# Weights converted at the start of an attention, MLP and expert kernel: exponents rebased by ScalarE, a normalisation's factor kept in a PSUM bank, and sixteen of the lower parts made by TensorE with identities

## The chip, the core and the metric

One core of one Trainium2 chip. The metric is the device time of one execution in microseconds (us). TensorE multiplies matrices into PSUM (eight banks, of which this kernel shares some), VectorE and ScalarE work element by element from SBUF and PSUM, GpSimd does so from SBUF alone, and SyncE starts transfers. In the profile's rows the engines are called PE, PEld (the load of TensorE's weights), DVE (VectorE), ACT (ScalarE), POOL (GpSimd) and SP (SyncE).

## The reference

Eight batches of 576 positions. First an attention without scores between positions, in eight heads of 64; its result, seen as 576 x 512, goes through a layer normalisation and an MLP of 512 to 2048 to 512 with a residual; then two of four small causal attentions are chosen for each position and mixed.

```python
q_s = softmax(q, axis=-1);  k_s = softmax(k, axis=seq)
kv = np.einsum('bhsd,bhse->bhde', k_s, v)
x = np.einsum('bhsd,bhde->bhse', q_s, kv)          # to (8, 576, 512)
xn = (x - mu) / np.sqrt(var + 1e-06) * g_ln
x = x + np.maximum(xn @ w_ch1, 0.0) @ w_ch2        # 512 -> 2048 -> 512
...                                                # top 2 of 4 experts of causal attention
```

## The kernel before

A batch is worked on in two halves of 288 columns. A unit is a pair of heads, four to a batch: its `k` and `q` are loaded, the exponentials taken, `q` is turned by products with an identity (`pq`), the product `pkv` is made and scaled into `kvw`, and a product of each half (`po`, plain fp32 while the unit is one of the first eight) is copied into `xT` by ScalarE. Norm is the layer normalisation of a half: GpSimd adds up the four parts of `xT` (`x_sum`), ScalarE and VectorE split the sum in two (`lnsum`), TensorE takes the mean of it (`pmu`), VectorE subtracts it (`xc`), ScalarE squares (`sq`), the same again gives the variance (`pvar`), three operations on ScalarE and two on VectorE (`refine`) give the factor, `scale` multiplies with it and with the gain, and ScalarE and VectorE split the outcome into a high and a lower part (`xhl`).

The MLP's matrices come in blocks of 128 rows by 512 as 64-bit floats. Each block is turned by `Wide.pieces` into a float32 that is split into a high part (f32r, the form that TensorE takes in one pass) and a lower part; three products (high with high, high with low, low with high) make one exact enough product. Block 2f is the part of the first matrix for step f (`w1_f`), block 2f+1 that of the second (`w2_f`). A step of the MLP is twelve products into `psh`, ReLU and split into `hh` by ScalarE and VectorE, and twelve products into four accumulators `acc0` to `acc3`.

The function `start` lays out batch 0's units, its norms and its first pass through steps 0 to 11 (in two chunks, 0 to 6 and 7 to 11, each for both halves), the conversion of blocks 0 to 23, and batch 1's units and norms. It names every operation with its engine, an assumed cost and what it depends on; rings say how many tiles or banks of a kind there are and who has to be done before the next one is handed out (`y`: two PSUM banks; `t`: four tiles of 128x512, in which blocks are converted and `x_sum` is kept; `raw`: four raw blocks). A greedy planner makes one order of it for each engine, and `in_order` holds every engine to that order. Later batches follow a fixed pattern; the last eight blocks are converted in the last pass by `Wide.step`. `CDVE` names the blocks whose lower part VectorE makes; GpSimd makes the others.

The pieces of a block, in the kernel's own words (the raw block's `low` and `high` are the two words of each number):

```python
nc.scalar.activation(t.bitcast(F32), high.bitcast(F32), AF.Abs)                                  # size
nc.vector.tensor_scalar(t, t, TINY, None, op0=ALU.max)                                           # least
nc.vector.tensor_scalar(t, t, 3, 0x3FFFFFF8, op0=ALU.logical_shift_left, op1=ALU.bitwise_and)    # shift
nc.scalar.activation(low, low.bitcast(U32), AF.Copy, scale=2.0 ** -29)                           # rest
nc.vector.scalar_tensor_tensor(box[0], high, -0x40000000, box[0], ...)                           # sign
nc.gpsimd.tensor_tensor(box[0], box[0], low, op=ALU.add)                                         # whole
nc.scalar.activation(h, box[0].bitcast(F32), AF.Copy)                                            # big
eng.tensor_tensor(lo, box[0].bitcast(F32), raw(h), op=ALU.subtract)                              # small
```

Of the kernel before, what the change touches and what calls it, by code (L numbers as in the profile page):

```python
# [7 lines left out]
F32 = mybir.dt.float32  # L8
# [18 lines left out]

WHOLE, KPOOL, QACT = 8, (0, 1, 5, 6, 7), (0, 1, 6, 7)

CDVE = (1, 4, 7, 8, 9, 14, 16, 17, 18, 20, 21)  # L30

DIRECT = ((0, 0),)

# [9 lines left out]
UNIT_AT, UNIT_GAP = (0, 1, 2, 4, 5, 7), 4  # L43
NORM_AT, NORM_GAP = (0, 2, 4, 6, 8, 10), 8

TINY = 2.0 ** -15 * 1.125


def weave(main, side):
# [80 lines left out]
def tile_kernel(ctx: ExitStack, tc: tile.TileContext, q, k, v, g_ln, w1, w2, w_gate, wq, wk, wv, wo, out):  # L130
# [25 lines left out]
    def raw(ap):  # L156
        return ap.bitcast(F32)
# [15 lines left out]
    def mm(o, lhsT, rhs, start, stop):  # L173
        nc.tensor.matmul(o, lhsT, rhs, start=start, stop=stop)  # L174
# [22 lines left out]
    mean_r = const.tile([P, P], F32R, name="mean_r")  # L197
    nc.vector.memset(raw(mean_r), 1.0 / DM)
    mean_mat = raw(mean_r)
    eps6 = const.tile([P, 1], F32, name="eps6")  # L200
    nc.vector.memset(eps6, 1e-6)
    g_sb = const.tile([P, NDC], F32, name="g_sb")
# [11 lines left out]
    class Wide:  # L214
# [18 lines left out]
        def pieces(self):  # L233


            r, h, lo = self.now()
            n = self.at
            self.at += 1
            low, high = r[:, :, 0], r[:, :, 1]
            box = []  # L240

            def size():
                t = self.pool_t.tile([P, DM], I32, tag="t", name="w_t", bufs=TB)
                box.append(t)
                nc.scalar.activation(t.bitcast(F32), high.bitcast(F32), AF.Abs)

            def least():
                t = box[0].bitcast(F32)
                nc.vector.tensor_scalar(t, t, TINY, None, op0=ALU.max)

            def shift():
                t = box[0]
                nc.vector.tensor_scalar(t, t, 3, 0x3FFFFFF8, op0=ALU.logical_shift_left, op1=ALU.bitwise_and)

            def rest():
                nc.scalar.activation(low, low.bitcast(U32), AF.Copy, scale=2.0 ** -29)

            def sign():
                nc.vector.scalar_tensor_tensor(box[0], high, -0x40000000, box[0], op0=ALU.bitwise_and,  # L259
                                               op1=ALU.bitwise_or)  # L260

            def whole():
                nc.gpsimd.tensor_tensor(box[0], box[0], low, op=ALU.add)  # L263

            def big():
                nc.scalar.activation(h, box[0].bitcast(F32), AF.Copy)

            def small():
                eng = nc.vector if n in CDVE else nc.gpsimd
                eng.tensor_tensor(lo, box[0].bitcast(F32), raw(h), op=ALU.subtract)  # L270
                while len(self.tiles) < min(n + 1 + self.ahead, len(self.blocks)):
                    self.load()

            return size, least, shift, rest, sign, whole, big, small

        def now(self):
            while len(self.tiles) <= self.at:
# [2 lines left out]

        def step(self):
            if self.at < len(self.blocks):
                for piece in self.pieces():
                    piece()

    def fc_blocks(f, w1t, w2t):
# [305 lines left out]
    class Norm:  # L592
# [37 lines left out]
        def less(self, c, n):  # L630
            if c == 0:
                self.xc = lp.tile([P, NDC, T], F32, tag="xc", name="xc")
            nc.vector.tensor_tensor(self.xc[:, c:c + n], self.xs[:, c:c + n],
                                    self.pmu[:, None].to_broadcast([P, n, T]), op=ALU.subtract)
# [12 lines left out]
        def refine(self):  # L647

            r0, t = (self.sq[:, i] for i in (1, 2))
            nc.vector.scalar_tensor_tensor(t, self.pvar, 1e-6, t, op0=ALU.add, op1=ALU.mult)  # L650
            nc.vector.scalar_tensor_tensor(t, t, 3.0, r0, op0=ALU.subtract, op1=ALU.mult)

        def scale(self, c):
            xc = self.xc[:, c]
            nc.vector.scalar_tensor_tensor(xc, xc, g_sb[:, c:c + 1], self.sq[:, 2], op0=ALU.mult, op1=ALU.mult)

        def high(self, c, n):
            if c == 0:
# [167 lines left out]
    def start():  # L826
# [117 lines left out]
        def norm(b, h):  # L944
# [7 lines left out]
            def mean(nm, x, done, add_, buf):  # L952
                if direct:
                    ps = op = None
                    for c in range(NDC):
                        op = A((nm, c), PE_, 490, lambda c=c: u.mean_direct(nm, x, c), [done[c], op])
                        ps = ps or op
                    return ps, op
                op = None
                for c in range(1, NDC):  # L960
                    op = A((nm, "add", c), POOL, 750, lambda c=c: add_(c), [op, done[0], done[c]])
                    if c == 1 and buf:
                        op0 = op
                hi = A((nm, "high"), ACT, 330, u.sum_high, [op])
                lo = A((nm, "low"), DVE, 370, u.sum_low, [hi])
                if buf:
                    op0.take(buf, lo)
                ps = A((nm, "mean"), PE_, 240, lambda: u.mean(nm), [lo])
                hi.take("lnsum", ps)
                return ps, ps  # L970

            first, last = mean("pmu", lambda: u.xs, kp, u.add_x, "t")
            less, sq = [], []
            for c in range(0, NDC, n):
                less += [A(("less", c), DVE, 370 if direct else 670, lambda c=c: u.less(c, n), [last, less[-1] if less else None])] * n
# [2 lines left out]
            first, last = mean("pvar", lambda: u.sq, sq, u.add_sq, None)  # L978
            root = A("root", ACT, 1000, u.root, [last])
            fine = A("fine", DVE, 800, u.refine, [root, at["g2"]])  # L980
            first.take("m" if direct else "y", fine)
            sc, lo = [], None
            his = []
            for c in range(NDC):
                sc.append(A(("sc", c), DVE, 430, lambda c=c: u.scale(c), [fine]))
                if (c + 1) % n == 0:
                    hi = A(("hi", c), ACT, 330 if direct else 570, lambda c=c: u.high(c + 1 - n, n), sc[c + 1 - n:] + his[-1:])
                    his.append(hi)
                    lo = A(("lo", c), DVE, 370 if direct else 670, lambda c=c: u.low(c + 1 - n, n), [hi, lo])
            less[0].take("xc", lo)  # L990
            sq[0].take("sq", sc[-1])
            at["hl", b, h] = lo

            his[0].take("xhl", *([at["lastf", h]] if b == 0 else ()))
# [3 lines left out]
        for k in range(nblocks):  # L998
            box = []
            live.append(box)  # L1000
            A = lambda nm, eng, cost, fn, deps: add(("w", k, nm), eng, cost, fn, deps)

            def one(i, box=box):
                if not box:
                    box.extend(wide.pieces())
                box[i]()

            g = lambda i, one=one: (lambda: one(i))
            ld = add(("w", k, "ld"), SP, 1450, wide.load, [at.get(("w", k - 1, "ld"))], lat=1100)
            c0 = A(0, ACT, 520, g(0), [at.get(("w", k - 1, 0)), ld])  # L1010
            c1 = A(10, DVE, 340, g(1), [c0])
            c1 = A(1, DVE, 340, g(2), [c1])
            c2 = A(2, ACT, 520, g(3), [c0])
            c3 = A(3, DVE, 600, g(4), [c1])
            c5 = c4 = A(4, POOL, 1220, g(5), [c2, c3])
            c6 = A(6, ACT, 520, g(6), [c4])
            c7 = A(7, *((DVE, 600) if k in CDVE else (POOL, 1220)), g(7), [c6, at.get(("w", k - 1, 7))])
            c0.take("t", c7)
            ld.take("raw", c5)

# [595 lines left out]
```

## Time and profile before

| | |
|---|---|
| median of 3 runs | 1355.34 us (1354.69 to 1357.6) |
| the profiled execution | 1356.32 us, its span 1354.6 us |
| mean granted clock of TensorE | 0.992 |
| TensorE busy | 1297.1 us (96%) |
| VectorE busy | 889.6 us (66%) |
| ScalarE busy | 687.5 us (51%) |
| GpSimd busy | 342.4 us (25%) |
| TensorE in 40 slices of the span, tenths | 5678 and then 35 times 9, at the end 7 |

The shares are means over the whole execution. A slice is 34 us long. Only the first four slices and the last show TensorE with room, so what happens there is read from windows and timelines of the first 164 us and not from the shares. The first `psh` of the MLP begins at 46.73 us; the stages below are cut there and at later groups of products. A row of a timeline is a run of equal instructions on one engine; behind it stands in brackets how long the engine was idle before it and which operation ended that. Matmuls are pipelined, so a row's length includes the drain of its last one; the distance between starts tells what a group takes.

### The profile page before, as it was taken

Reading aid. Unit: us, or ns where it says so; the run is one execution under the profiler, and the core shown is the slowest. Engines: PE = TensorE matmul, PEld = TensorE weight load, DVE = VectorE, ACT = ScalarE, POOL = GpSimd, SP = SyncE. Lnnn points to the kernel's source line nnn. Section 1 sums busy time; section 2 is a strip of 40 time slices with the busy share of each in tenths; the row PEclk is TensorE's granted clock in tenths of the full one; section 3 lists DMA queues with packets and bytes.
Section 4 is the critical chain, followed back from the end, with each engine's and each line's share of the span. In section 5 each row is a group of like instructions: output and inputs, shape, how many; then the busy total and the mean of one; then the engine's idle time right before and its main releaser. Section 6 shows DMA issues by size and latency. Waiting matters only on the chain.

```text
span 1354.6 us, 26863 instructions
## 1 busy us (share of the span) xinstructions
PE 1297.1 (96%) x9932; PEld 1255.8 (93%) x9932; DVE 889.6 (66%) x2602; ACT 687.5 (51%) x1802; POOL 342.4 (25%) x445
## 2 busy tenths in 40 slices
PE   5678999999999999999999999999999999999997
PEld 3578999999999999999999999999999999999995
DVE  7999564654645656456472238777768677776785
ACT  7667443434343434344442135656556656565666
POOL 5756413122131221212240002111211111121211
PEclk9898999999999999999999999999999999999999
DMA  8655232331322324215112023323232332423021
GB/s 228 200 174 150 80 96 72 112 93 50 110 75 94 85 72 114 75 53 156 64 34 47 1 83 121 107 83 106 85 94 90 90 98 62 118 84 86 23 67 56
DMA packets 136772, 124.84 MB, mean 92 GB/s; under 512 B 84160, under 2 KB 124096, under 8 KB 133056
## 3 DMA queue, kind: packets, MB, share of 16 engines
q1 hardware_dynamic: 126176, 97.16, 25.6%
q10 hardware_dynamic: 10464, 25.95, 5.3%
q8 instruction: 79, 1.29, 0.4%
q14 instruction: 53, 0.43, 0.1%
HBM read 74.07 MB, written 35.39 MB: 81 GB/s over the span
## 4 chain that ended last, share of the span: by engine, by line
PE 70%; DVE 4%; DMA 2%; ACT 1%; issue 1%; SPq 0%; POOL 0%; ACTq 0%; DVEq 0%
PE psh L174 21%; PE acc L174 14%; PE psqk L174 7%; PE psc L174 7%; PE pssc L174 4%; PE py L174 4%; PE psv L174 4%; PE pso L174 3%; PE pst L1401 2%; PE po L174 1%; DMA q<-in_q_dram 1%; PE pkv L174 1%; PE pst L1450 1%; DMA k<-in_k_dram 0%; PE pq L510 0%
## 5 line engine op out<-in xcount | busy, mean ns | idle before, releaser
L174 PE MATMUL psh<-xhl,w 128*128 128x288 f32 x3072 | 470.4, 299 | 5.2 <-DVE w L270 2.2
L174 PEld LDWEIGHTS psh<-xhl,w 128*128 128x128 f32 x3072 | 429.7, 190 | 8.6 <-DVE w L270 2.5
L174 PE MATMUL acc<-hh,w 128*128 128x288 f32 x2400 | 371.4, 299 | 10.0 <-DVE hh L714 8.9
L174 PEld LDWEIGHTS acc<-hh,w 128*128 128x128 f32 x2400 | 335.6, 189 | 14.4 <-DVE hh L714 10.9
L714 DVE SCALAR_TENSOR_TENSOR hh<-psh,hh 128x288 fp32r<-128x288 f32 x200 | 90.5, 453 | 159.5 <-ACT hh L711 158.2
L711 ACT ACTIVATE hh<-psh 128x288 fp32r<-128x288 f32 x200 | 81.6, 408 | 170.0 <-PE psh L174 165.2
L1389 POOL TENSOR_SCALAR sm<-sm,st,lg 128x128 f32<-128x128 f32 (+3 forms) x128 | 80.3, 637 | 273.6 <-DVE st L1386 99.1
L174 PE MATMUL psqk<-x,wqk 128*128 128x288 f32 x768 | 112.6, 298 | 0.5 <-DVE lg L1289 0.3
L174 PEld LDWEIGHTS psqk<-x,wqk 128*128 128x128 f32 x768 | 104.7, 188 | 1.8 <-PE pst L1401 0.8
L174 PE MATMUL psc<-hb,w 128*128 128x288 f32 x672 | 100.5, 299 | 0.0
L1377 ACT ACTIVATE sm<-sm,st 128x128 f32<-128x128 f32 (+2 forms) x144 | 83.7, 583 | 17.9 <-DVE st L1369 16.7
L174 PEld LDWEIGHTS psc<-hb,w 128*128 128x128 f32 x672 | 92.4, 189 | 0.3
L1420 ACT ACTIVATE aTh<-pst 128x128 fp32r<-128x128 f32 (+5 forms) x254 | 79.2, 334 | 24.7 <-PE pst L1401 12.2
L1369 DVE CUSTOM_DVE_ANT_0 sm<-pssc,mask 128x128 f32<-128x128 f32 (+2 forms) x144 | 67.7, 482 | 32.2 <-PE pst L1401 19.9
L1421 DVE TENSOR_TENSOR aTl<-pst,aTh 128x384 fp32r<-128x384 f32 (+4 forms) x222 | 82.0, 382 | 9.8 <-ACT aTh L1420 7.1
L476 POOL TENSOR_TENSOR qe<-q,sm 128x320 f32<-128x320 f32 x64 | 47.5, 763 | 87.5 <-PE pkv L515 78.2
L611 POOL TENSOR_TENSOR sq<-sq 128x288 f32<-128x288 f32 x45 | 37.3, 828 | 109.4 <-ACT sq L639 107.4
L174 PE MATMUL py<-aTh,vv 128*128 128x320 f32 (+4 forms) x228 | 58.4, 275 | 1.6 <-DVE yf L1473 0.9
L425 POOL TENSOR_TENSOR q<-q,sm 128x640 f32<-128x640 f32 x28 | 35.9, 1283 | 91.2 <-DVE sm L422 86.2
L174 PE MATMUL pssc<-k,q 128*128 128x128 f32 (+3 forms) x256 | 58.0, 326 | 0.5 <-DVE st L1369 0.5
L263 POOL TENSOR_TENSOR w_t<-w_t,wraw 128x512 int32<-128x512 int32 x32 | 45.2, 1414 | 51.6 <-DVE w_t L259 13.3
L174 PE MATMUL psv<-wvg,x 128*128 128x260 f32 (+1 forms) x384 | 54.3, 285 | 0.0
(174 smaller groups left out, 2115.8 us busy)
## 6 DMA issues: line engine op xcount, KB each, us to landing
wraw<-in_moe_w_ch_dram SPq DMA_DIRECT2D x32, 512.0 KB, 3.9
xn_d<-xhl ACTq DMA_DIRECT2D x14, 1152.0 KB, 5.0
xhl<-xn_d SPq DMA_DIRECT2D x14, 1152.0 KB, 5.1
xp_d<-xT ACTq DMA_DIRECT2D x16, 576.0 KB, 3.6
k<-k SPq DMA_DIRECT2D x32, 288.0 KB, 3.5
k<-in_k_dram SPq DMA_DIRECT2D x32, 256.0 KB, 2.9
q<-in_q_dram SPq DMA_DIRECT2D x32, 256.0 KB, 3.6
out_dram<-ot SPq DMA_DIRECT2D x32, 256.0 KB, 2.0
```

The lines of the kernel that those rows point to most:

```text
L174: nc.tensor.matmul(o, lhsT, rhs, start=start, stop=stop)
L263: nc.gpsimd.tensor_tensor(box[0], box[0], low, op=ALU.add)
L425: nc.gpsimd.tensor_tensor(self.q3, self.q3, self.sm[:, 0, :, None].to_broadcast([P, 2 * NCH, D]), op=ALU.subtract)
L476: nc.gpsimd.tensor_tensor(self.qe[:, :, j, :], self.qt[:, j], self.sm[:, 2, j * NCH:(j + 1) * NCH, None].to_broadcast([P, NCH, D]), op=ALU ...
L611: nc.gpsimd.tensor_tensor(self.t, self.t, self.sq[:, c], op=ALU.add)
L711: nc.scalar.activation(self.hh[:, 0], self.ps, AF.Relu)
L714: nc.vector.scalar_tensor_tensor(self.hh[:, 1], self.ps, 0.0, raw(self.hh[:, 0]), op0=ALU.max, op1=ALU.subtract)
L1369: nc.vector.tensor_tensor_reduce(out=sm[:m, c0:c1], in0=o_, in1=msk, scale=1.0, scalar=3e38 if n == 0 else st[:m, j, 0:1], op0=ALU.add, op ...
L1377: nc.scalar.activation(sm[:m, :w], sm[:m, :w], AF.Exp, bias=st[:m, j, last:last + 1], scale=-1.0, accum_out=st[:m, j, 2:3])
L1389: nc.gpsimd.tensor_scalar(sm[:m, :w], sm[:m, :w], st[:m, j, 3:4], self.gate()[:, j:j + 1], op0=ALU.mult, op1=ALU.mult)
L1420: nc.scalar.activation(oh, from_, AF.Copy)
L1421: nc.vector.tensor_tensor(ol, from_, raw(oh), op=ALU.subtract)
```

## The change

Four edits. First, `size` becomes a ScalarE copy with the scale 2^-112, which rebases the exponent, so that `least` goes, the shift is a shift alone, and `sign` brings in the sign bit only. Second, for sixteen of the first 24 blocks the lower part is made by TensorE: an fp32 product of the identity with the block and an f32r product of the negative identity with its high part, into one of the two `y` banks (`plo`, 128x512), which ScalarE (six blocks) or VectorE (ten) copies out; the other eight lower parts are on GpSimd. Third, of the last eight blocks VectorE makes two lower parts in place of three. Fourth, the factor of a norm is written into the bank of its variance and read from there by the four scales, so the bank is held until the last scale and `sq` is free earlier; one dependence between the two norms of a later batch is added.

```diff
-CDVE = (1, 4, 7, 8, 9, 14, 16, 17, 18, 20, 21)
+CDVE = (1, 4)
+TENS_ACT = (8, 11, 14, 17, 20, 23)
+TENS_DVE = (1, 4, 6, 7, 9, 13, 16, 18, 19, 21)
...
+    minus = const.tile([P, P], F32R, name="minus")
+    nc.vector.tensor_scalar(minus, ident, -1.0, None, op0=ALU.mult)
...
-                nc.scalar.activation(t.bitcast(F32), high.bitcast(F32), AF.Abs)
-
-            def least():
-                t = box[0].bitcast(F32)
-                nc.vector.tensor_scalar(t, t, TINY, None, op0=ALU.max)
+                nc.scalar.activation(t.bitcast(F32), high.bitcast(F32), AF.Copy, scale=REBASE)
...
-                nc.vector.tensor_scalar(t, t, 3, 0x3FFFFFF8, op0=ALU.logical_shift_left, op1=ALU.bitwise_and)
+                nc.vector.tensor_scalar(t, t, 3, None, op0=ALU.logical_shift_left)
...
-                nc.vector.scalar_tensor_tensor(box[0], high, -0x40000000, box[0], op0=ALU.bitwise_and,
+                nc.vector.scalar_tensor_tensor(box[0], high, -0x80000000, box[0], op0=ALU.bitwise_and,
...
+            def less():
+
+                ps = psy(f"plo{n}")
+                box.append(ps)
+                mm(ps[:, :DM], ident, box[0].bitcast(F32), True, False)
+                mm(ps[:, :DM], minus, h, False, True)
+
+            def take(act):
+                ps = box[1][:, :DM]
+                if act:
+                    nc.scalar.activation(lo, ps, AF.Copy)
+                else:
+                    nc.vector.tensor_copy(lo, ps)
...
-                for piece in self.pieces():
+                for piece in self.pieces()[:7]:
...
-            nc.vector.scalar_tensor_tensor(t, t, 3.0, r0, op0=ALU.subtract, op1=ALU.mult)
+            nc.vector.scalar_tensor_tensor(self.pvar, t, 3.0, r0, op0=ALU.subtract, op1=ALU.mult)
...
-            nc.vector.scalar_tensor_tensor(xc, xc, g_sb[:, c:c + 1], self.sq[:, 2], op0=ALU.mult, op1=ALU.mult)
+            nc.vector.scalar_tensor_tensor(xc, xc, g_sb[:, c:c + 1], self.pvar, op0=ALU.mult, op1=ALU.mult)
...
+            if b and h:
+
+                at["ln", b, h, ("pmu", "high")].deps.append(at["ln", b, h - 1, ("pvar", "mean")])
...
-            first.take("m" if direct else "y", fine)
...
+            first.take("m" if direct else "y", sc[-1])
...
-            sq[0].take("sq", sc[-1])
+            sq[0].take("sq", fine)
...
-            c7 = A(7, *((DVE, 600) if k in CDVE else (POOL, 1220)), g(7), [c6, at.get(("w", k - 1, 7))])
+            if k in TENS_ACT + TENS_DVE:
+                pl = A(8, PE_, 1130, g(7), [c6])
+                c7 = A(7, *((ACT, 600) if k in TENS_ACT else (DVE, 600)), g(8, k in TENS_ACT), [pl])
+                pl.take("y", c7)
+            else:
+                c7 = A(7, *((DVE, 600) if k in CDVE else (POOL, 1220)), g(6), [c6, at.get(("w", k - 1, 7))])
```

Since the planner's order follows from costs and dependences, operations move on every engine. Two places of it follow. In a row stand the line, the operation, what it writes and reads (with a running number behind each name) and the size; x3 is three equal rows in a run.

On TensorE, late in the first pass (the last two steps of batch 0's second chunk for half 0; `po7` is the last product of batch 1's last unit, for half 0 and then half 1), the order before is this:

```order
L174 MATMUL acc3_1456<-hh_1587,w2_10_536 128x288 x3
L174 MATMUL acc0_1453<-hh_1620,w2_11_538 128x288 x3
L174 MATMUL acc1_1454<-hh_1620,w2_11_538 128x288 x3
L174 MATMUL acc2_1455<-hh_1620,w2_11_538 128x288 x3
L174 MATMUL acc3_1456<-hh_1620,w2_11_538 128x288 x3
L174 MATMUL pmu_1638<-lnsum_1622,mean_r_83 128x288 x2
L174 MATMUL psh_1641<-xhl_955,w1_7_529 128x288 x12
L174 MATMUL psh_1660<-xhl_955,w1_8_531 128x288 x12
L174 MATMUL po7_1682<-qT7_1534,kvw1_140 128x288
```

and in the changed kernel this:

```order
L177 MATMUL acc3_1394<-hh_1522,w2_9_543 128x288 x3
L177 MATMUL psh_1571<-xhl_602,w1_10_544 128x288 x12
L177 MATMUL po7_1584<-qT7_1525,kvw1_142 128x288
L177 MATMUL po7_1591<-qT7_1525,kvw1_142 128x288
L177 MATMUL pmu_1600<-lnsum_1594,mean_r_83 128x288 x2
L177 MATMUL plo21_1625<-w_t_1598,ident_78 128x512
L177 MATMUL plo21_1625<-w2_10_545,minus_85 128x512
L177 MATMUL plo23_1634<-w_t_1611,ident_78 128x512
L177 MATMUL plo23_1634<-w2_11_547,minus_85 128x512
L177 MATMUL acc0_1391<-hh_1586,w2_10_545 128x288 x3
```

The conversions of blocks 21 and 23 now stand behind `po7` and the mean on TensorE, and the products of steps 10 and 11 stand behind them; before, those products stood ahead of the mean, and both halves of `po7` stood apart.

On VectorE, the same place in the changed kernel (`w_t_1598`, `w_t_1606` and `w_t_1611` are blocks 21, 22 and 23; the line of the subtraction of the mean is 649, of shift and sign 255 and 261):

```order
L730 SCALAR_TENSOR_TENSOR hh_1586<-psh_1571,hh_1586 128x288
L634 TENSOR_TENSOR lnsum_1594<-x_sum_1343,lnsum_1594 128x288
L649 TENSOR_TENSOR xc_1603<-xT_1168,pmu_1600 128x576 x2
L255 TENSOR_SCALAR w_t_1598<-w_t_1598 128x512
L261 SCALAR_TENSOR_TENSOR w_t_1598<-wraw_1137,w_t_1598 128x512
L255 TENSOR_SCALAR w_t_1606<-w_t_1606 128x512
L261 SCALAR_TENSOR_TENSOR w_t_1606<-wraw_1379,w_t_1606 128x512
L255 TENSOR_SCALAR w_t_1611<-w_t_1611 128x512
L261 SCALAR_TENSOR_TENSOR w_t_1611<-wraw_1473,w_t_1611 128x512
L288 CAST w2_10_545<-plo21_1625 128x512
L634 TENSOR_TENSOR lnsum_1665<-sq_1618,lnsum_1665 128x288
```

where the order before had no block left to convert:

```order
L714 SCALAR_TENSOR_TENSOR hh_1620<-psh_1593,hh_1620 128x288
L618 TENSOR_TENSOR lnsum_1622<-x_sum_1398,lnsum_1622 128x288
L732 TENSOR_TENSOR xT_344<-xT_344,acc0_1453 128x288
L633 TENSOR_TENSOR xc_1655<-xT_867,pmu_1638 128x576 x2
L732 TENSOR_TENSOR xT_344<-xT_344,acc1_1454 128x288
```

The last three blocks have moved from ahead of the norm to behind its subtraction.

## Rows read from the trace of the kernel before

**Rows 1.** Windows; columns: stretch, us, each engine's busy time (instructions), clock, DMA.

```profile
20.73:34.90 14.17, 10.16 (x76) 6.92 (x75) 12.39 (x25) 13.86 (x30) 7.72 (x7) 1.00 0.81 233
46.73:62.90 16.17, 14.50 (x100) 13.72 (x100) 16.07 (x27) 11.85 (x24) 10.80 (x9) 0.76 0.53 187
62.90:91.09 28.19, 16.84 (x108) 15.60 (x105) 27.09 (x37) 16.97 (x35) 17.29 (x13) 0.94 0.52 158
91.09:163.34 72.25, 68.25 (x517) 64.91 (x515) 57.36 (x107) 43.16 (x118) 39.33 (x35) 0.95 0.41 129
163.34:240.00 76.66, 76.66 (x639) 75.72 (x638) 42.99 (x95) 30.48 (x65) 20.13 (x24) 1.00 0.29 82
84.69:91.09 6.40, 6.40 (x37) 6.40 (x38) 5.57 (x9) 4.22 (x9) 1.29 (x1) 0.73 0.30 108
116.45:122.05 5.60, 5.60 (x21) 4.92 (x21) 4.37 (x9) 5.06 (x10) 3.30 (x3) 0.50 0.59 189
```

**Rows 2.** Timeline of TensorE, 84 to 164 us: start, length, operation, count, idle before.

```profile
84.69 2.66 PE L174 MATMUL acc<-hh,w 128*128 128x288 f32 x11 [4.37 <-DVE hh L714]
...
105.57 0.55 PE L510 MATMUL pq<-ident,qe 112*128 112x112 f32 x4
...
116.45 1.33 PE L174 MATMUL po<-qT,kvw 128*128 128x288 f32 x2 [2.75 <-ACT kvw L537]
...
138.91 0.65 PE L174 MATMUL po<-qT,kvw 128*128 128x288 f32 x2
...
140.98 3.59 PE L174 MATMUL acc<-hh,w 128*128 128x288 f32 x24
...
161.74 1.76 PE L174 MATMUL acc<-hh,w 128*128 128x288 f32 x12
163.34 0.43 PE L174 MATMUL pmu<-lnsum,mean_r 128*128 128x288 f32 x2
```

**Rows 3.** Lines of VectorE, 14 to 131 us: count, busy us, mean ns, idle before.

```profile
L259 DVE SCALAR_TENSOR_TENSOR w_t<-wraw,w_t 128x512 int32<-128x512 int32 x23 | 20.0, 870 | 0.4
L249 DVE TENSOR_SCALAR w_t<-w_t 128x512 f32<-128x512 f32 x23 | 18.0, 783 | 1.4 <-ACT w_t L245 1.4
L253 DVE TENSOR_SCALAR w_t<-w_t 128x512 int32<-128x512 int32 x23 | 17.4, 758 | 0.3
L270 DVE TENSOR_TENSOR w<-w_t,w 128x512 fp32r<-128x512 f32 x10 | 11.4, 1152 | 0.2 <-ACT w L266 0.2
...
L655 DVE SCALAR_TENSOR_TENSOR xc<-xc,g_sb,sq 128x288 f32<-128x288 f32 x8 | 6.4, 842 | 0.0
```

**Rows 4.** Timeline of VectorE and GpSimd at the first scales, 43 to 47 us.

```profile
43.08 1.29 POOL L263 TENSOR_TENSOR w_t<-w_t,wraw 128x512 int32<-128x512 int32 x1
43.83 0.45 DVE L650 SCALAR_TENSOR_TENSOR sq<-pvar,sq 128x288 f32<-128x288 f32 x1
...
44.89 2.17 DVE L655 SCALAR_TENSOR_TENSOR xc<-xc,g_sb,sq 128x288 f32<-128x288 f32 x3
```

**Rows 5.** Timeline of ScalarE, VectorE and GpSimd around the last unit.

```profile
130.04 0.69 DVE L259 SCALAR_TENSOR_TENSOR w_t<-wraw,w_t 128x512 int32<-128x512 int32 x1
...
134.59 1.29 POOL L263 TENSOR_TENSOR w_t<-w_t,wraw 128x512 int32<-128x512 int32 x1 [1.15 <-ACT xT L557]
...
142.27 1.56 POOL L606 TENSOR_TENSOR x_sum<-x_sum,xT 128x288 f32<-128x288 f32 x2
...
143.87 0.45 ACT L615 ACTIVATE lnsum<-x_sum 128x288 fp32r<-128x288 f32 x1 [2.21 <-POOL x_sum L606]
144.34 0.46 DVE L618 TENSOR_TENSOR lnsum<-x_sum,lnsum 128x288 fp32r<-128x288 f32 x1 [1.56 <-ACT lnsum L615]
...
145.29 1.42 DVE L633 TENSOR_TENSOR xc<-xT,pmu 128x576 f32<-128x576 f32 x2
```

**Rows 6.** Timeline of TensorE and VectorE in the last pass, 703 to 712 us.

```profile
704.77 0.41 DVE L253 TENSOR_SCALAR w_t<-w_t 128x512 int32<-128x512 int32 x1
...
710.30 1.32 PE L174 MATMUL acc<-hh,w 128*128 128x288 f32 x8 [1.94 <-DVE hh L714]
```

More of the change, by code (lines that the diff above doesn't have):

```diff
@@ L44 @@
 NORM_AT, NORM_GAP = (0, 2, 4, 6, 8, 10), 8
-TINY = 2.0 ** -15 * 1.125
+REBASE = 2.0 ** -112
 def weave(main, side):
@@ L272, in small @@
                     self.load()
-            return size, least, shift, rest, sign, whole, big, small
+            def less():
[9 more added lines that the diff above has]
+                    nc.vector.tensor_copy(lo, ps)
+            return size, shift, rest, sign, whole, big, small, less, take
         def now(self):
@@ L1001, in start, with one @@
             A = lambda nm, eng, cost, fn, deps: add(("w", k, nm), eng, cost, fn, deps)
-            def one(i, box=box):
+            def one(i, *a, box=box):
                 if not box:
                     box.extend(wide.pieces())
-                box[i]()
-            g = lambda i, one=one: (lambda: one(i))
+                box[i](*a)
+            g = lambda i, *a, one=one: (lambda: one(i, *a))
             ld = add(("w", k, "ld"), SP, 1450, wide.load, [at.get(("w", k - 1, "ld"))], lat=1100)
             c0 = A(0, ACT, 520, g(0), [at.get(("w", k - 1, 0)), ld])
[L1011 to L1016, printed above, removed]
-            c7 = A(7, *((DVE, 600) if k in CDVE else (POOL, 1220)), g(7), [c6, at.get(("w", k - 1, 7))])
+            c1 = A(1, DVE, 340, g(1), [c0])
+            c2 = A(2, ACT, 520, g(2), [c0])
+            c3 = A(3, DVE, 600, g(3), [c1])
+            c5 = c4 = A(4, POOL, 1220, g(4), [c2, c3])
+            c6 = A(6, ACT, 520, g(5), [c4])
+            if k in TENS_ACT + TENS_DVE:
[4 more added lines that the diff above has]
+                c7 = A(7, *((DVE, 600) if k in CDVE else (POOL, 1220)), g(6), [c6, at.get(("w", k - 1, 7))])
             c0.take("t", c7)
```

## The prediction

> **What bounds the kernel now.** I read the page's slices first, then windows, then timelines. The slices show TensorE full from the fifth one on, so the conversion of weights in the first 163 us stands where TensorE still waits. The windows give the stages [rows 1]. From 163.34 on TensorE is busy 76.66 of 76.66 us at clock 1.00: added products there cost their full time and freed vector time gives nothing. Before that it is short of work: 14.50 of 16.17 us, then 16.84 of 28.19, then 68.25 of 72.25. VectorE is busy 16.07 and 27.09 us of the first two of these, so until 91 us VectorE's list ends last; after 91 us it has slack (57.36 of 72.25). The timeline of TensorE names single waits [rows 2]: 4.37 us for a `hh` at 84.69, 2.75 us for a `kvw` at 116.45. After a long wait the granted clock falls: 0.73 over 84.69 to 91.09, 0.50 over 116.45 to 122.05, which costs 1.7 and 2.8 us [rows 1]. So there is at most 11.35 us of waiting in the third stage, 4.0 in the fourth, 1.7 in the second, some 8 of slow clock (the 0.76 of the second stage, 3.9, among it), and the start before 46.73, to be won; against it stands what TensorE is given.
>
> **What TensorE pays.** Twelve f32r products of 288 columns take 163.34 − 161.74 = 1.60 us, 0.133 each. A `po` is one plain fp32 product of 288 columns; with the twelve behind it it takes 140.98 − 138.91 = 2.07, so 0.47 to 0.48 alone [rows 2]. One identity pair (`plo`: fp32 of 512 columns, then f32r of 512) is therefore 0.86 + 0.24 = 1.10 us. Sixteen are added; the first two fall before the first `psh`, where TensorE waits anyway. Fourteen on the path: 15.4 us.
>
> Lower bound for the identity product: the transposes with the same identity at 105.57, four of 112 columns in 0.55 us including the last one's drain, about 0.10 each by their starts, so 0.45 for 512 and 0.69 for the pair [rows 2]. Upper bound: 1.10, as `po`. I take 1.10, because `plo` is a plain product with accumulation like `po`, no transpose. [...]
>
> **What VectorE gets back.** Per block, the `least` goes (L249, mean 0.783 us), and ten lower parts (L270, 1.152) [rows 3]; ten copies of a PSUM bank come in. No copy of 512 columns out of PSUM is in the trace: a PSUM reader of 288 columns takes 0.45 [rows 4] and a subtraction of 576 columns 0.71 [rows 5], so 0.45 to 0.71; I take 0.70. Counted in the order, ahead of the first lower part of `xhl` six L249 and one L270 go and two copies come; ahead of the eighth `hh` fifteen L249 and five L270 go, six copies and three blocks' shift and sign (0.758 + 0.870) come.
>
> The normalisation's factor in a bank: the scales at 44.89 take 2.17/3 = 0.72 while a GpSimd addition runs beside them, and 0.84 in the mean; the operation with one operand in PSUM at 43.83 takes 0.45 although GpSimd's addition of 43.08 covers it [rows 3, 4]. So a scale is 0.45 to 0.84; I take 0.46, as it becomes an operation of that kind. Eight scales in the ramp: 3.0 us less. [...]
>
> ScalarE's rebasing (Copy for Abs) costs nothing: the same pass over 512 columns. The bank held until the last scale costs nothing after the ramp, as the next mean comes many microseconds later.
>
> **The sum, stage by stage**, against the profiled execution's own 1356.3 us (the median of the runs is 1.0 lower).
>
> 1. Front, to 46.73. ScalarE is busy 13.86 of 14.17 us from 20.73 to 34.90 [rows 1] with the same list, so the last results of the front's units come no earlier. After that VectorE's list up to the first scales loses two L249 and an L270 and gains two copies: −1.6 − 1.15 + 1.4 = **−1.3** (bounds 0, and −4.5 if all that VectorE is spared since 14 us counted: 6 × 0.78 + 1.15 − 1.4).
> 2. 46.73 to 62.90: two pairs come in (+2.2), a transposition and a `pkv` move out (−1.3), one copy is waited for (+0.5); the clock of 0.76 stays, since TensorE still stands idle ahead of the first `psh`: **+1.4**.
> 3. 62.90 to 91.09: now 28.19. Work at full rate: eight groups of twelve 12.7, the mean 0.3, the moved unit's products 1.3, four pairs 4.4; I leave 1.7 for waits, since VectorE's list there is shorter by about the 11.35 us that TensorE waits (15 × 0.78 + 5 × 1.15 − 6 × 0.70 − 3 × 1.63 + 8 × 0.38 = 11.5). 20.4: **−7.8**.
> 4. 91.09 to 163.34: eight pairs +8.8, moved products +1.2; present waits (4.0) and slow clock (2.8) go, if nothing takes their place: **+3.2**.
> 5. What takes their place is in the order of TensorE. Behind `po7` come the mean of batch 1's first half and then `plo21` and `plo23`, ahead of all remaining `acc` and `psh`. Block 21's tile is the one that `x_sum` held, and its shift stands behind the subtraction of the mean. So from `po7`'s end a chain runs with TensorE idle but for a second `po7` and the mean [rows 5]: ScalarE's copy and its split 0.45 each, GpSimd's last add 0.78 between them, VectorE 0.46, mean 0.4, subtraction 1.42, shift 0.41 [rows 6], sign 0.69, GpSimd's sum 1.29, hand-overs 0.3: 6.65, less 0.75 of TensorE's own: 5.9. `plo23` then waits for two more of GpSimd's sums, 1.5 (both just follow) to 3.1 (VectorE's pairs blocked beside them), and ScalarE's high part behind squares, up to 0.9. 7.4 to 9.9, I take 8.6. The clock falls after it as after the 4.37 and 2.75 waits (1.7 and 2.8): 2.4. **+11.0**.
> 6. Chains sum → high part → pair → copy in 91 to 132, where TensorE can catch up with one: **+1.2** (0 to 6).
> 7. Last pass: block 7 of the last eight leaves VectorE, where its lower part stood ahead of a `hh` that TensorE waited 1.94 for [rows 6]: **−2.0**.
>
> Together −1.3 + 1.4 − 7.8 + 3.2 + 11.0 + 1.2 − 2.0 = +5.7: 1362.1 own time, **1361.1** in the runs' median. 0.2% is 2.7 us, about what a measurement of this kernel can tell from no change.
>
> **Rivals.**
>
> *Identity products are cheap (0.20), not slower.* Place: TensorE's fourteen pairs. At the transposes' price a pair is 0.69, 5.8 us less: 1355.3; at one pass for both products 0.47, 8.8 less: 1352.3. It ends on the fast side below about 0.50 us a pair. For it: the same identity as TensorE's stationary operand at 105.57. Against: `po`'s plain fp32 product.
>
> *TensorE waits at each pair (0.16), slower.* Each of the six pairs from 91 to 132 stands behind GpSimd's sum of the same block, and GpSimd is busy half of that stage (39.33 of 72.25 [rows 1]). About 1 us each with the clock behind it, 6 more than taken: 1367.
>
> *The front comes forward by all that VectorE is spared (0.08).* −4.5 instead of −1.3: 1357.9. For it: VectorE is busy through the front; against: ScalarE's 13.86 of 14.17.
>
> *As summed (0.56)*: own range 1356.5 to 1366, from the tail's 7.4 to 9.9 us, the clock's 0 to 2.8, the front's bounds and the copies' 0.45 to 0.71.
>
> **Numbers.** Faster by over 0.2%: 0.12 of the cheap products, 0.02 of the front and 0.01 of the sum, 0.15. Within: 0.08 + 0.03 + 0.07 = 0.18. Slower: 0.48 of the sum, 0.16 and 0.03, 0.67. The range reaches from the cheap products' case, 1353.0, to just above the waits' case, 1368.0; some 0.13 is left below and 0.06 above.
>
> **What would show it.** A record pair of `plo` of 1.1 us between its start and the next product's; copies at 0.7; scales at 0.46 whatever GpSimd does; the first `psh` at 45.4; the last `psh` of the third stage done about 8 us before 91; then one wait of 6 us or more behind `po7` on `plo21` and another on `plo23`, with a lower clock after. It is wrong if that hole is missing or short, if the third stage keeps its waits, or if a pair is at 0.7 or below.

## The result, and the profile after

The changed kernel took 1374.9 us in the median of 4 runs (1373.85 to 1375.67), the kernel before 1355.41 beside it: ratio 1.0137, 95% interval 1.0123 to 1.0151. It is slower, as forecast, but by 19.5 us and not by 5.7. Two executions among all runs had a mean granted clock of only 0.559 and 0.595 (2130.6 us in the run that frees the bank, 1973.99 us of the kernel before) and are left out of what follows. The profiled execution has a span of 1373.0 us at a mean clock of 0.985, 18.4 more than before.

The stages of the changed kernel by windows (the columns are those of [rows 1]; the bounds are the same products as there as far as the order allows):

```profile
46.97:62.17 15.20, 13.44 (x66) 11.85 (x67) 15.06 (x22) 9.09 (x18) 11.47 (x10) 0.70 0.67 220
62.17:92.09 29.92, 22.77 (x140) 18.73 (x139) 21.94 (x40) 22.51 (x59) 14.04 (x13) 0.89 0.47 147
92.09:116.77 24.68, 24.68 (x193) 23.60 (x192) 10.64 (x24) 10.27 (x23) 7.43 (x7) 1.00 0.52 159
116.77:148.00 31.23, 26.88 (x183) 22.23 (x182) 15.15 (x33) 19.05 (x52) 15.16 (x15) 0.95 0.41 115
148.00:171.71 23.71, 16.49 (x76) 12.71 (x75) 10.98 (x18) 9.97 (x20) 8.97 (x9) 0.71 0.00 1
```

The third row, 92.09 to 116.77, is a stage that the kernel before does not have: TensorE full, VectorE busy 10.64 us and GpSimd 7.43 of 24.68. In the two rows behind it TensorE is short of work: it is busy 26.88 of 31.23 and 16.49 of 23.71 us, the last at a clock of 0.71. TensorE's waits from 40 to 200 us, the four largest of them (in total, times, longest):

```profile
PE plo L177 <- POOL w_t L265: 5.7, 2, 4.1
PE pkv L531 <- ACT qT L516: 4.0, 1, 4.0
PE pkm L458 <- DVE cm L450: 2.6, 1, 2.6
PE acc L177 <- DVE hh L730: 2.4, 1, 2.4
```

Single places on TensorE's timeline:

```profile
46.97 0.61 PE L177 MATMUL psh<-xhl,w 128*128 128x288 f32 x1 [2.34 <-ACT xhl L676]
...
59.46 1.02 PE L177 MATMUL plo<-w_t,ident 128*128 128x512 f32 x2
59.92 0.79 PE L177 MATMUL plo<-w,minus 128*128 128x512 f32 x1
60.55 1.78 PE L177 MATMUL acc<-hh,w 128*128 128x288 f32 x12
...
80.14 0.47 PE L531 MATMUL pkv<-ident,qe 128*128 128x128 f32 x1 [4.00 <-ACT qT L516]
...
83.42 2.05 PE L177 MATMUL plo<-w_t,ident 128*128 128x512 f32 x2 [1.50 <-DVE xc L671]
...
127.59 2.82 PE L177 MATMUL acc<-hh,w 128*128 128x288 f32 x11 [2.41 <-DVE hh L730]
...
148.01 1.13 PE L177 MATMUL po<-qT,kvw 128*128 128x288 f32 x4
150.50 0.40 PE L177 MATMUL pmu<-lnsum,mean_r 128*128 128x288 f32 x1 [1.36 <-ACT lnsum L631]
...
155.54 2.08 PE L177 MATMUL plo<-w_t,ident 128*128 128x512 f32 x2 [4.05 <-POOL w_t L265]
...
159.66 2.08 PE L177 MATMUL plo<-w_t,ident 128*128 128x512 f32 x2 [1.61 <-POOL w_t L265]
```

The pair of 59.46 takes until 60.55, 1.09 us. The hole stands where the order put it, behind `po7` of 148.01: 1.36 for the mean, 4.05 for block 21, 1.61 for block 23. In the pairs there the fp32 product's two records take 2.08 us in place of 1.02: the granted clock over them is 0.50, over the pair of 59.46 it is 1.00. VectorE's groups from 14 to 171 us (columns as in [rows 3]):

```profile
L261 DVE SCALAR_TENSOR_TENSOR w_t<-wraw,w_t 128x512 int32<-128x512 int32 x24 | 23.9, 996 | 0.6
L255 DVE TENSOR_SCALAR w_t<-w_t 128x512 int32<-128x512 int32 x24 | 13.1, 545 | 9.1 <-ACT w_t L251 9.0
...
L288 DVE CAST w<-plo 128x512 fp32r<-128x512 f32 x10 | 6.9, 685 | 1.0 <-PE plo L177 1.0
...
L671 DVE SCALAR_TENSOR_TENSOR xc<-xc,g_sb,pvar 128x288 f32<-128x288 f32 x8 | 3.8, 507 | 0.1
```

To see where the time went I summed the columns of TensorE's records in both traces, `plo` left out, and looked when each kernel had done the work that the kernel before has done at a given time. The lag of the changed kernel, and what the prediction's steps add up to there:

```
kernel before at, us     50     90    140    150    650    740   1300
lag measured, us        0.7    3.7   11.1   22.8   20.1   16.6   18.6
lag predicted, us      -1.3   -7.7   -3.3    7.7    7.7    5.7    5.7
```

A lag below zero means that the changed kernel is ahead. The sums are of one execution each, and good to some 0.4 us.

From 140 to 150 the hole costs 11.7 (predicted 11.0). Ahead of it 14 us are missing in the prediction, 11 of them before 90 us and the rest by 140.

### The profile page after: what moved, and what is told of

Same layout as the page of the kernel before. It is cut to its first block, busy times and chain, and to the rows that moved or that the text cites. A ratio compares the mean times of both kernels' runs of the same rounds, so it can differ in the third digit from the quotient of the medians.

```text
span 1373.0 us, 26951 instructions
## 1 busy us (share of the span) xinstructions
PE 1318.6 (96%) x9980; PEld 1267.2 (92%) x9980; DVE 860.3 (63%) x2569; ACT 692.8 (50%) x1808; POOL 332.7 (24%) x441
## 4 chain that ended last, share of the span: by engine, by line
PE 84%; DVE 6%; ACT 3%; DMA 3%; issue 1%; SPq 1%; POOL 1%; ACTq 0%; POOLq 0%; DVEq 0%
PE psh L177 27%; PE acc L177 21%; PE psqk L177 7%; PE psc L177 7%; PE pssc L177 4%; PE py L177 4%; PE psv L177 4%; PE pso L177 3%; PE pst L1424 2%; PE po L177 2%; DMA q<-in_q_dram 1%; PE pkv L177 1%; DVE w_t L261 1%; PE plo L177 1%; PE pq L526 1%
## 5 line engine op out<-in xcount | busy, mean ns | idle before, releaser
L1392 DVE CUSTOM_DVE_ANT_0 sm<-pssc,mask 128x128 f32<-128x128 f32 (+2 forms) x144 | 67.7, 482 | 34.4 <-PE pst L1424 20.1
```

The lines of the kernel that those rows point to most:

```text
L1392: nc.vector.tensor_tensor_reduce(out=sm[:m, c0:c1], in0=o_, in1=msk, scale=1.0, scalar=3e38 if n == 0 else st[:m, j, 0:1], op0=ALU.add, op ...
```

## The experiments

The first theory, from the waits above: three losses. The bank that holds the factor keeps TensorE at 80.14 and 83.42; blocks 21 to 23 wait for tiles behind `x_sum` (the hole); and the pairs cost their own 15.4 us. The rivals stand with each run. Times are medians; where a run stood beside the kernel before, that was at 1355 to 1356.2.

**The bank and the hole.** The factor back in SBUF, the planner told as before, so the start's order stays:

```diff
-            nc.vector.scalar_tensor_tensor(self.pvar, t, 3.0, r0, op0=ALU.subtract, op1=ALU.mult)
+            nc.vector.scalar_tensor_tensor(t, t, 3.0, r0, op0=ALU.subtract, op1=ALU.mult)
...
-            nc.vector.scalar_tensor_tensor(xc, xc, g_sb[:, c:c + 1], self.pvar, op0=ALU.mult, op1=ALU.mult)
+            nc.vector.scalar_tensor_tensor(xc, xc, g_sb[:, c:c + 1], self.sq[:, 2], op0=ALU.mult, op1=ALU.mult)
```

> The changed kernel with the factor back in SBUF; the planner is told as before that the bank is held, so that the order of the start stays. Theory 1 (the bank that the factor holds until the last scale blocks TensorE at 75.6 to 85 us: waits of 4.0 and 1.5 us and a lower clock behind them): 4 to 9 us faster than the changed kernel, 1366 to 1371. Rival (that bank is free only when the factor is ready anyway, and ScalarE's list makes both it and the turned q late): under 1.5 us faster, 1373 to 1375.

1376.26 us (median of three), ratio to before 1.0148 (1.0127 to 1.017): not faster. The waits at that place did shrink, from 4.00 and 1.50 us to 1.87 and 1.18, and came back at the next step, 1.31 of it at 92.16 for a `hh`. That its `hh` and weights stood behind longer scales is my estimate, from the means of 842 ns with the factor in SBUF in the kernel before [rows 3] and 507 ns with it in the bank; no row of this run shows one. TensorE's timeline of this run:

```profile
78.19 0.33 PE L531 MATMUL pkv<-ident,qe 128*128 128x128 f32 x1 [1.87 <-DVE sq L666]
...
80.44 1.45 PE L177 MATMUL plo<-w_t,ident 128*128 128x512 f32 x2 [1.18 <-ACT qT L516]
...
92.16 0.40 PE L177 MATMUL acc<-hh,w 128*128 128x288 f32 x1 [1.31 <-ACT hh L727]
```

So the bank is not what costs, and the first part of the theory fell here. The second edit, batch 1's sums start after block 23 has its tile:

```diff
                     op = A((nm, "add", c), POOL, 750, lambda c=c: add_(c), [op, done[0], done[c]])
+                    if b and buf and c == 1:
+                        op.deps.append(at["w", 2 * FSPLIT - 1, 0])
```

> The changed kernel with one dependence more for the planner: the sums of batch 1's norms, which take two of the four tiles of 128x512, start after block 23 has its tile. Theory (the hole behind po7 of 4.1 and 1.6 us of waits on GpSimd's sums, 1.4 on the mean, with the low clock behind it, comes from blocks 21 to 23 waiting for those tiles): 8 to 12 us faster than the changed kernel, 1363 to 1367. Rival (TensorE is out of work there because the conversion as a whole is late, and only its name changes): under 3 us faster, 1372 to 1375.

1363.22 us, 1.005 (1.0035 to 1.0065): 11.7 faster, the hole is gone (the last window below is full), and the stage before it still has TensorE at 25.20 of 30 us:

```profile
115.00:145.00 30.00, 25.20 (x148) 19.77 (x147) 18.44 (x33) 20.98 (x56) 14.04 (x12) 0.94 0.38 114
145.00:175.00 30.00, 30.00 (x233) 29.00 (x233) 16.97 (x36) 12.97 (x29) 11.75 (x14) 1.00 0.20 70
```

Both together, and both with the planner told that the bank is free earlier (`first.take("y", fine)` again, `sq` held until the last scale):

> Both edits of the two runs before together, the planner still told that the bank is held. If the two losses are apart in time and add: the sum of both gains within 2 us, 1355 to 1362 by the theories, 1370 to 1375 by the rivals.

> As the run before, but the planner is told that the bank is free when the factor is in SBUF, and places the turn of unit 4 by that. Theory (the planner's placement of that turn behind the variance costs as well): 1 to 4 us faster than the run before. Rival (the placement costs nothing): within 1 us of it.

1366.03 (1.007) and 1366.73 (1.0078): some 3 us slower than the late sums alone, so there are no two gains that add. With the sums late the factor's bank is a gain of about 3 us, its hold included.

**Each edit alone, on the kernel before.** The rebase alone (`size` a copy with 2^-112, no `least`, the new masks), the factor in the bank alone, the last eight blocks' edit alone, and TensorE's lower parts with the last eight blocks' edit:

> The kernel before with the first edit alone: ScalarE rebases the exponent, VectorE's least goes, 24 operations of 0.78 us. Theory (VectorE's list bounds the first 91 us): 3 to 8 us faster than before, 1347 to 1352. Rival (TensorE waits there for chains over ScalarE and GpSimd, whatever VectorE is spared): within 2.7 us of before.

> The kernel before with the factor in the bank alone. Theory (the held bank costs TensorE waits in the ramp, as in the changed kernel): 2 to 6 us slower than before, 1357 to 1361. Rival (without the pairs there are banks enough, and the scales are shorter by 0.38 us each): 0 to 3 us faster.

> The kernel before with the third edit alone: block 7 of the last eight has its lower part made by GpSimd. By the prediction 2.0 us faster; by the traces of both kernels, in which about 3.5 us of waits between 640 and 725 us went, up to 3.5 faster; rival (GpSimd's later lower part makes TensorE wait for the weights instead): no change or slower.

> The kernel before with the third edit and TensorE's lower parts alone (sixteen pairs of 1.1 us, the least still on VectorE). Theory (the pairs cost their own 15.4 us on TensorE, and give back at most the 11 us that TensorE waited for VectorE before 91 us, with the hole behind po7 as in the changed kernel): 8 to 16 us slower than before, 1363 to 1371. Rival (the loss is the bank's and not the pairs'): within 4 us of before.

The rebase: 1351.11, ratio 0.9967 (0.9954 to 0.998), 5.1 us faster, but not where the theory had it. By the sum of columns its lag is −0.1 us at 90 and at 150, and −5.7 from 740 on: nothing in the start, 1.2 in the passes and 4.3 in the last pass, where the waits of [rows 6] are gone. In the start TensorE is no further on, with VectorE freed of 24 operations; its waits stand at other places:

```profile
63.87 6.11 PE L174 MATMUL acc<-hh,w 128*128 128x288 f32 x23 [3.35 <-DVE hh L710]
...
77.45 0.47 PE L438 MATMUL pkm<-ident,cm 128*128 128x128 f32 x1 [4.08 <-DVE cm L430]
```

The bank: 1358.3, 1.0019 (1.0009 to 1.0028), 2.1 us slower than the kernel before beside it. By the columns it loses nothing in the start (−0.7 at 150) and 4 us in the passes between; why there is open. The last blocks' edit: 1355.75, 0.9998 (0.9989 to 1.0008), nothing; the wait of [rows 6] stands there unchanged:

```profile
710.63 1.32 PE L174 MATMUL acc<-hh,w 128*128 128x288 f32 x8 [1.94 <-DVE hh L714]
```

TensorE's lower parts: 1380.44, 1.0182 (1.0165 to 1.0198), 24.2 us slower, more than the theory gave. The loss comes with the pairs' edit.

**What sixteen pairs cost.** With the late sums: pairs for blocks up to 13 alone, for blocks 14 to 23 alone (`TENS_ACT`, `TENS_DVE` and `CDVE` cut accordingly), and each pair made twice:

```diff
-                mm(ps[:, :DM], ident, box[0].bitcast(F32), True, False)
-                mm(ps[:, :DM], minus, h, False, True)
+                for _ in range(2):
+                    mm(ps[:, :DM], ident, box[0].bitcast(F32), True, False)
+                    mm(ps[:, :DM], minus, h, False, True)
```

> The kernel with the sums late (1363.2 us), with TensorE's lower parts for blocks up to 13 alone; of blocks 14 to 23 VectorE makes 14, 16, 17, 18, 20 and 21 and GpSimd the others, as in the kernel before. Theory (a pair costs TensorE its 1.1 us wherever TensorE is full, and from 91 us on it is): 6 to 9 us faster than with all sixteen, 1354 to 1357. Rival (the late pairs are cheap, since VectorE and GpSimd are relieved for them): within 2.7 us of it.

> The same with TensorE's lower parts for blocks 14 to 23 alone; of blocks 0 to 13 VectorE makes 1, 4, 7, 8 and 9 and GpSimd the others. If the prediction's third step held (VectorE's list ends last before 91 us, so the early pairs buy back more than they cost): 2 to 6 us slower than with all sixteen, 1365 to 1369. Theory now (the early pairs buy nothing): 3 to 7 us faster, 1356 to 1360.

> The kernel with the sums late, in which each pair is made twice into the same bank; the planner is not told, so the order of the start stays. Theory (fourteen pairs lie on the path): 13 to 16 us slower than with each pair once, 1376 to 1379. Rival (the pairs lie in time in which TensorE would wait anyway): under 6 us slower.

1352.67 (0.9979), 1352.12 (0.997) and 1369.81 (1.0106). Leaving out either half takes some 11 us away, more than either theory gave, and twice the products cost 6.6 us: less than the 13 to 16 of the theory, a little more than the rival allows. So 0.4 of the added pairs' own time on TensorE (sixteen of 1.09 us) is paid in this order, and not all of it. A run with more lower parts on VectorE, and three to see what none, and who makes the rest, is worth (the `CDVE` set with 6, 11, 13, 19 and 23 added; no pairs; late pairs with 6, 11 and 13 added):

> The kernel before with the first edit, and VectorE makes the lower part of five blocks more (6, 11, 13, 19 and 23) in place of GpSimd; the last eight blocks as in the changed kernel. If the chain over GpSimd is what TensorE waits for in the first 163 us: 2 to 6 us faster than with the first edit alone, 1345 to 1349. Rival (what is freed on one engine is filled with work of later units, and the start stays as long): within 2.7 us of 1351.1.

> The kernel with the sums late, without any lower part by TensorE; VectorE and GpSimd share all 24 as in the kernel before. If eight pairs are free and the second eight cost 11 us: within 2.7 us of 1352. If each pair costs its own time and the halves only met a better order: 5 to 9 us faster than either half, 1343 to 1347.

> The same with five lower parts moved from GpSimd to VectorE (6, 11, 13, 19, 23). If GpSimd's share bounds the start also here: 3 to 6 us faster than without the move. Rival (with the bank VectorE's list is short enough only for what it has): within 2.7 us of it.

> TensorE's lower parts for blocks 14 to 23 alone, and of blocks up to 13 VectorE makes 1, 4, 6, 7, 8, 9, 11 and 13. If the early stage is bound by GpSimd and the late pairs are cheap: 3 to 6 us faster than the run of the late pairs, 1346 to 1349. Rival (the late pairs cost what is won early): within 2.7 us of 1352.1.

The rebase with five more lower parts on VectorE: 1345.91, 0.9931 (0.9919 to 0.9944), 5.2 faster than the rebase alone, and by the columns 4.6 of that stand already at 90 us: a freed VectorE is worth something in the start once it takes work off GpSimd. No pairs: 1352.33 (0.9978; the runs spread from 1346.87 to 1355.72), so that in the whole time eight pairs of either kind cost next to nothing. The others 1347.81 (0.9952) and 1349.3 (0.9957).

The columns say more than the whole times. At 150 us (one execution of each) the kernel without pairs is 4.6 us ahead of the kernel before, with either half of the pairs 0.6 and 1.0 behind it, and with all sixteen (sums late) 10.2 behind. In the start, then, either half costs 5 to 6 us and the two together 15. The whole times meet because the kernel without pairs loses 2.5 us between 180 and 400, as the kernel with the bank alone does; why is open.

**Who holds the tiles.** `size`, the first piece of a block, takes one of the four tiles; for the planner the block gives it back when its lower part is copied. The rows do not print block numbers; these follow from the order of each engine's list, which the kernel fixes. ScalarE's timeline has these of its `size` in the changed kernel:

```profile
93.32 0.68 ACT L251 ACTIVATE w_t<-wraw 128x512 f32<-128x512 f32 x1
...
119.00 0.67 ACT L251 ACTIVATE w_t<-wraw 128x512 f32<-128x512 f32 x1
...
150.35 0.66 ACT L251 ACTIVATE w_t<-wraw 128x512 f32<-128x512 f32 x1
```

The first of these rows is block 17, the next 18, the last 21 (22 and 23 follow at 151.46 and 152.57): from 93.32 to 119.00 no block begins. Blocks 14 to 17 hold the four tiles. Three have their pairs at 115.42, 123.59 and 135.52 us on TensorE, because the planner orders by due time and the weights of steps 7 and 8 are due late; the fourth is on GpSimd, behind a unit:

```profile
115.42 1.02 PE L177 MATMUL plo<-w_t,ident 128*128 128x512 f32 x2
...
123.59 1.12 PE L177 MATMUL plo<-w_t,ident 128*128 128x512 f32 x2 [0.80 <-ACT xT L573]
...
135.52 1.12 PE L177 MATMUL plo<-w_t,ident 128*128 128x512 f32 x2 [0.38 <-DVE w L288]
```

The kernel before stops there too, for 14.7 us (91.00 to 105.69). Tiles are short earlier as well. Block 10 begins when block 6 has its lower part: in the kernel before at 58.71, behind GpSimd, and in the changed kernel at 64.36, behind the copy of the pair of 59.46, which stood in VectorE's list for 3 us. The first two rows are of the kernel before, the others of the changed one:

```profile
56.94 1.74 POOL L270 TENSOR_TENSOR w<-w_t,w 128x512 fp32r<-128x512 f32 x1
58.71 0.70 ACT L245 ACTIVATE w_t<-wraw 128x512 f32<-128x512 f32 x1 [0.84 <-POOL w L270]
...
63.51 0.67 DVE L288 CAST w<-plo 128x512 fp32r<-128x512 f32 x1
64.36 0.67 ACT L251 ACTIVATE w_t<-wraw 128x512 f32<-128x512 f32 x1
```

Three runs: a pair is placed as soon as it is ready (the first edit), five tiles in place of four, and five tiles in the kernel before:

```diff
                 pl = A(8, PE_, 1130, g(7), [c6])
+                pl.soon = True
...
     free, taken, todo = {}, {}, list(ops)
+    for op in ops:
+        if getattr(op, "soon", False):
+            op.late = RUSH
```

```diff
-TB, MIDB, AHEAD = 4, 4, 2
+TB, MIDB, AHEAD = 5, 4, 2
```

> The changed kernel; the planner places a pair as soon as it is ready, whatever its step's due time. Theory (pairs that wait for their turn on TensorE hold the four tiles, so that conversion stops from 93 to 119 us, and both the hole behind po7 and the second eight pairs' price come from that): 15 to 22 us faster than the changed kernel, 1353 to 1360, with no hole behind po7. Rival (the pairs' own 15 us are the price, wherever they stand): the hole's 12 us at most, 1363 or more.

> The changed kernel with five tiles of 128x512 in place of four, the planner told. Theory (the tiles are what is short): 12 us faster by the hole that goes, and 2 to 6 more, 1357 to 1363. Rival (the hole is one of dependences and not of tiles): within 3 us of the changed kernel.

> The kernel before with five tiles. If four tiles were enough there, since its lower parts follow at once: within 2.7 us of before. If not: 3 or more faster, and the fifth tile is a gain of its own.

1352.68 (0.9993, 0.9983 to 1.0003), 1353.81 (0.9986, 0.9973 to 0.9999) and 1361.64 (1.0057, 1.0041 to 1.0073). With the sixteen pairs themselves unchanged, their earlier place takes 22.2 us away, and a fifth tile 21.1, more than the 12 and 2 to 6 forecast; without pairs a fifth tile is no gain, it costs 6 to 7. Either edit moves operations on every engine, since the planner starts from it anew. ScalarE's last two `size` in the run with pairs placed at once, on its timeline (line 254 there):

```profile
98.91 0.65 ACT L254 ACTIVATE w_t<-wraw 128x512 f32<-128x512 f32 x1
...
101.64 0.66 ACT L254 ACTIVATE w_t<-wraw 128x512 f32<-128x512 f32 x1
```

The last block begins at 101.64 and not at 152.57. Its windows behind that:

```profile
90.00:115.00 25.00, 23.07 (x141) 18.27 (x141) 16.28 (x27) 18.28 (x50) 13.36 (x11) 0.93 0.32 100
115.00:145.00 30.00, 29.80 (x257) 27.81 (x256) 15.57 (x38) 17.54 (x53) 13.70 (x15) 1.00 0.43 116
145.00:175.00 30.00, 29.06 (x218) 28.66 (x217) 14.96 (x32) 11.10 (x24) 5.65 (x7) 1.00 0.22 80
```

No hole: TensorE is busy 29.80 and 29.06 of 30 us in the last two. All sixteen pairs lie ahead of them; the last begins at 111.1 us.

The stop from 93 to 119 is a sign of the shortage, but not the whole price. The run with five tiles has one as long, on ScalarE's timeline:

```profile
85.39 0.65 ACT L251 ACTIVATE w_t<-wraw 128x512 f32<-128x512 f32 x1
...
110.55 0.65 ACT L251 ACTIVATE w_t<-wraw 128x512 f32<-128x512 f32 x1
```

and TensorE is as short of work behind it. What differs stands ahead of the stop. The windows from 46.50 to 90 and from 115 to 145 of the changed kernel, the same of the run with five tiles, and the first of them of the run with pairs placed at once:

```profile
46.50:90.00 43.50, 34.13 (x193) 29.00 (x194) 36.36 (x59) 29.97 (x73) 25.59 (x22) 0.81 0.51 159
115.00:145.00 30.00, 25.65 (x169) 20.42 (x168) 16.29 (x37) 19.55 (x54) 16.93 (x17) 0.94 0.45 123
...
46.50:90.00 43.50, 39.24 (x242) 35.19 (x243) 39.95 (x67) 31.28 (x60) 28.36 (x22) 0.94 0.71 227
115.00:145.00 30.00, 24.41 (x162) 18.89 (x161) 16.62 (x28) 15.18 (x32) 16.95 (x16) 0.94 0.32 89
...
46.50:90.00 43.50, 40.11 (x229) 34.35 (x230) 40.53 (x66) 31.52 (x60) 24.81 (x22) 0.93 0.65 203
```

By the columns the changed kernel is 3.7 us behind the kernel before at 90 us; with five tiles it is 8.4 ahead and with pairs placed at once 7.3 ahead. So about half of the 22 us lies before 90 us, and most of the rest is the hole behind `po7`, which neither run has (with five tiles TensorE is busy 29.99 of 30 us from 145 to 175). Block 10, which begins at 64.36 in the changed kernel, begins at 52.52 with five tiles and at 55.04 with pairs placed at once. That two so different edits give the same time back shows that the pairs' late place with four tiles is what cost; how much a new plan can do by itself, the 6 to 7 us of the fifth tile in the kernel before say. Which waits before 90 us carry the loss is shown for block 10 alone.

## Why the prediction was wrong

The direction was right, the size not: 19.5 against 5.7 us. Step by step:

The terms for single operations held. A pair takes 1.09 us (predicted 1.10), a copy out of the bank 0.685 (0.70), a scale 0.507 (0.46, between 0.45 and 0.84).

Step 5, the hole, was right in place and in size: 11.7 us measured between the same work, 11.0 predicted, and 11.7 came back when the sums were moved. The size has some luck in it: the waits were 7.0 us (1.36, 4.05 and 1.61) where 8.6 was taken, so that some 4.7, an estimate, are left for the lower clock behind them, where 2.4 was taken. Its cause was only half seen. I took `x_sum` as the holder of block 21's tile; the late sums show that this is enough to make the hole, but the pairs placed at once remove it without an edit to the sums. The conversion was late because pairs held the tiles, and the sums came to lie ahead of it.

Step 3 failed, and with it the prediction: between 50 and 90 us the lag grew by 3.0 where steps 2 and 3 have it shrink by 6.4, and these are 9 of the 14 us that are missing ahead of the hole (step 1 has 2, steps 4 and 6 have 3). Step 3 took 7.8 us off because VectorE's list "ends last until 91 us" and became 11.5 us shorter. The list did become shorter (busy 15.06 + 21.94 us from 46.97 to 92.09, where it was 16.07 + 27.09 from 46.73 to 91.09 [rows 1]), and TensorE got none of it: its lag grew to 3.7 at 90. The rebase alone says the same without any pair: 15 operations fewer, lag −0.1. So VectorE, busy as it was, did not alone end the chain; probably it was busy with later units' work, which the planner puts into free time. GpSimd is in the chain as well: five lower parts moved from it to VectorE bring 5.2 us. And what the step put at nothing is the wait for a tile. Where blocks get their tiles earlier, the same four edits do bring what it forecast: its sum has TensorE 7.7 us ahead at 90, and the runs with five tiles and with pairs placed at once are 8.4 and 7.3 ahead. No run separates what VectorE's and what GpSimd's shorter list gave there.

From 90 to 140 the lag grew by 7.4 where steps 4 and 6 have 4.4. Step 4 let 6.8 us of waits and slow clock vanish "if nothing takes their place"; between 116.77 and 148 the changed kernel waits 4.35 us again, one of them (2.41 at 127.59) for a `hh` that stands in VectorE's list behind the maximum of a `q` whose load had not landed:

```profile
126.36 0.82 DVE L438 TENSOR_REDUCE sm<-q 128x10 f32<-128x640 f32 x1 [3.37 <-DMA q<-in_q_dram]
```

The pairs' own time, on which the sum rested as a fixed cost of 15.4, is not what is paid in every order. Sixteen pairs placed at once leave the kernel no slower than it is without pairs (1352.68 and 1352.33, the latter with the sums late), and 4 us behind it at 150; twice the products cost 0.4 of their time. What I costed right as work was in large part hidden, and what I costed at nothing, the wait of later blocks for the four tiles that pairs keep, was the larger price: the same sixteen pairs, placed as soon as they are ready, bring the kernel from 1374.9 to 1352.7, and placed by due time as before, but with a fifth tile, to 1353.8.

Step 1: the first `psh` came at 46.97, 0.24 later, not 1.3 earlier. The two pairs that were to fall into waiting time stand between `po` and the mean on TensorE and their copies in VectorE's list; with late pairs only, the first `psh` is at 42.65. Which of the two delays it is not shown.

Step 7: −2.0 predicted, −3.5 measured (20.1 to 16.6), and for another reason. Block 7's edit alone does nothing; the rebase alone, which takes the `least` out of VectorE's list, gives 4.3 there.

Of the rivals, none named this. The slower one (a wait at each pair for GpSimd's sum) had the sign and the stage, but from 91 to 148 us TensorE waits at three pairs only, 0.80, 0.38 and 0.77 us, and none of these waits ends with GpSimd. Cheap identity products are ruled out by the 1.09 us, an early front by the first `psh`. Left open are the 4 us that the bank alone costs in the passes between, the 2.0 us that the changed kernel loses between 740 and 1300, and why a fifth tile makes the kernel before slower.

## What to carry to other kernels

When work moves to another engine, cost not only its time there but how long it keeps the buffers that feed it: write down for each shared tile when it is taken and when it is given back, in the new order. A planner that orders by due time lets an operation with a late due time wait while it holds a tile that early work needs; here it was worth 22.2 us to place such operations at once. And a busy engine is no proof that it bounds a stage: see which engine's freed time moves the next stage's first wait.

## What was not expected of the hardware

VectorE's operations did not all get shorter when its list did. The shift went from a mean of 0.758 us to 0.545, but the sign, with two operands in SBUF, from 0.870 to 0.996 [rows 3], while a copy out of PSUM takes 0.685. The means mix two kinds. A sign takes 0.69 us while GpSimd is idle and up to 1.69 beside one of its operations; of the changed kernel's two here, GpSimd's addition of 59.15 runs beside the first:

```profile
59.15 1.47 POOL L265 TENSOR_TENSOR w_t<-w_t,wraw 128x512 int32<-128x512 int32 x1
59.50 1.66 DVE L261 SCALAR_TENSOR_TENSOR w_t<-wraw,w_t 128x512 int32<-128x512 int32 x1
...
120.38 0.69 DVE L261 SCALAR_TENSOR_TENSOR w_t<-wraw,w_t 128x512 int32<-128x512 int32 x1
```

The copies out of PSUM (0.67 to 0.69) and the scales with one operand in PSUM (0.50 to 0.51) take the same with GpSimd beside them or not; a scale with both operands in SBUF, in the kernel before, takes 0.50 to 0.52 with GpSimd idle and up to 1.51 beside it. The shift, which reads one tensor from SBUF, varies as well, from 0.42 alone to as much as 1.36 beside GpSimd; why it does, no run here shows.
